# A planned TensorE stream: event waits counted in its instruction blocks, and tiling forms chosen by the tiling in force

## The chip, the cores and the metric

The kernel runs on one core of a Trainium2 chip (trn2). The metric is the time of one execution on the device in microseconds (us), as the median of several runs. Beside it stands one profiled execution, from which all rows and durations are taken; its times are in us unless marked ns.

## The reference

Two branches over the same input `x` (2048 tokens, 576 features) are mixed by a gate for each token.

```python
g = sigmoid((x * gate_w).sum(-1, keepdims=True))
a = A(x)      # recurrent, 64 segments of 32 tokens
b = B(x)      # full attention, 32 heads of 18 features
out = g * a + (1 - g) * b

# A: for each segment s (H = 32 heads of 128, M = 8 memory rows)
h = concat([mem, x_s])                     # 40 rows
q, k, v = h @ Wq, h @ Wk, h @ Wv           # 576 -> 32 x 128
p = softmax(mask(q @ k.T * scale))         # 40 x 40, each head
o = (p @ v) @ Wo
mem = o[:8]; out_s = o[8:]                 # the next segment needs mem

# B: qkv = x @ wqkv, softmax(q @ k.T * scale) @ v over 2048 x 2048, @ wo
```

The weights, inputs and the output are bfloat16. Branch A is a chain of 64 dependent segments, branch B is independent of it.

## The kernel before

**Tiling.** Features are cut in four pieces of 128 and a tail of 4 x 16 rows. Branch A's projections, one pair (q, k or v; half of the heads) at a time, are `Q0 Q1 K0 K1 V0 V1`: five groups of four matmuls, one for each group of 32 columns of TensorE's array ("column form", written 128\*32 in the profile), 512 wide, into `pvv` (L1255). The profile writes a matmul's form as active rows x columns: 128\*128 is the full form, 32\*128 the row form, 64\*128 the tall form.

**A segment** then goes: `pvv` is cast to `tm`; q and k are transposed by DMA (`tt`) and copied to `qk`; scores `psh` (`ph`, L1378, with the mask from `veil`, L1370); exponent on ACT (`xp`); sums over the keys `pss` (`sm`, L1402); reciprocal `rq`; the sums are spread to all rows `prb` (`bc`, L1428); the weights are multiplied (`nm`); values `pso` (`po`, L1450, tall form); copies to `ot`; output product `acc` (`op`, L1163); `oc`/`bd` prepare its first rows and `fold` (`fo`, L1507) turns them into the memory columns of the next segment's `ht` (`ph`, L1517). Only 32 of the 40 rows go through this path. The last 8 tokens of each segment are projected ahead in *last-token units* (`last_unit`, L1000 and L1004, into `pv`), two units a segment, for 16 segments at a time; their output product is `lo0`/`lo1` (`acc` from `otl`), once for four segments.

**Branch B** is 512 *visits*: four heads' scores at once in row form (`sb` and `sp`, L907), two exponents on ACT (`ex`, `ey`), and the values in column form (`ob`, L930). They are spread over the segments (`seg_gate`) to fill TensorE while a segment's chain waits.

**The order.** The kernel doesn't write its instructions in loops' order. Every step is added to a `Plan` with its engines, an assumed duration, dependencies, priority, tiling `mode`, PSUM banks it takes and gives, and, for TensorE, `pairs`, the number of its matmuls (each with a weight load). `Plan.run` is a list scheduler: it always places the step that can start first, with a priority among those within `near`, and `emit` then writes all instructions in that order. A change of TensorE's tiling is charged `SWITCH` = 0.105 us in the plan, and `rank` in `choose` adds the knob `switch` to the priority of a step in another tiling. `choose` waits for urgent steps by further knobs.

`TURNS` holds 65 seeds, one for each segment and one more; `turn` derives from a seed, through `factor`, a multiplier for the priority of each kind of step and for each of six knobs. They come from a search.

**Filler.** While branch B's accumulator is open and the plan sees TensorE idle for longer than 0.216 us plus the knob `gap`, it puts in a *warm* step: matmuls with zeros added onto `ob` (`warm_col`, L877, four 512 wide; `warm_full`, L883, one).

**Blocks.** `fetched` models that TensorE's instructions come in blocks of 128 pairs. `count` is the pairs placed so far; when a step crosses a block's end, it is set back until `FETCH` us after the last crossing:

```python
BLOCK, FETCH = 128, 3.75
for k in range(self.BLOCK - self.count % self.BLOCK, n + 1, self.BLOCK):
    at = start + dur * k / n + late
    late += max(0.0, self.block_end + self.FETCH - at)
    self.block_end = at
```

Event waits that the build puts into TensorE's stream as instructions of their own aren't in `count`.

**Forms.** Which form a step takes is fixed by constants, `LA_COL, SM_COL, BC_COL, FO_COL = False, True, True, True`: the sums, the spread and the fold in column form (4 x 3 matmuls), the last-token products of q and k in full form (5 matmuls of 128 columns for a part), those of v in column form except in the first group, before the segments.

Of the kernel before, what the change touches and what calls it, by code (L numbers as in the profile page):

```python
# [55 lines left out]
RANK = dict(RANKS[0])  # L56
TURNS = [
    7483491, 5720459, 7783898, 6678073, 6223742, 3115698, 6578494, 0, 354389, 7990747, 1981828, 1088679,
    6361070, 8635106, 9405432, 0, 1645198, 9020719, 1300847, 3314955, 2575603, 9878751, 9165885, 8658054,
    7165588, 8616252, 6219048, 2965226, 8978382, 6854479, 7325218, 5187600, 3485097, 1925321, 7771989,  # L60
    9649268, 8425308, 6353945, 3935120, 9399223, 8266427, 5356296, 6832100, 452821, 6190037, 6777369, 3367981,
    1424859, 9365357, 1390216, 6449117, 224178, 2255892, 1025974, 9211044, 7746781, 430414, 7144472, 1307610,
    6009236, 9165363, 683202, 7413963, 1206068, 9782046,
]
# [3 lines left out]

def factor(turn, k):
    h = (turn * 2654435761 + k * 40503 + 12345) & 0xFFFFFFFF  # L70
    h ^= h >> 15
    h = (h * 2246822519) & 0xFFFFFFFF
    h ^= h >> 13
    h = (h * 3266489917) & 0xFFFFFFFF
    h ^= h >> 16
    return FACTORS[(h >> 8) & 15] if turn and (h & 255) < 80 else 1.0

# [10 lines left out]
class Op:  # L88
# [3 lines left out]
        "engs", "dur", "fn", "deps", "prio", "mode", "take", "give", "tail",  # L92
        "eng", "start", "end", "left", "users", "name", "seq", "slots", "dmas", "kb", "use", "pairs", "kind",
    )
# [11 lines left out]
class Plan:  # L106
# [8 lines left out]
    WARM = 0.216  # L115
    BLOCK, FETCH = 128, 3.75
    ARRAY = {"col": 1.0, "row": 1.0, "full": 0.9, "half": 0.3, "tall": 0.35}
# [13 lines left out]
    def fetched(self, start, dur, n):  # L131

        late = 0.0
        for k in range(self.BLOCK - self.count % self.BLOCK, n + 1, self.BLOCK):
            at = start + dur * k / n + late
            late += max(0.0, self.block_end + self.FETCH - at)
            self.block_end = at
        self.count += n
        return late
# [24 lines left out]
    def add(  # L164
        self, name, engs, dur, fn, deps=(), prio=5.0, mode=None, take=(), give=(), tail=0.0, dmas=0, kb=0.0,
        use=None, pairs=4,
    ):
        op = Op(name, engs, dur, fn, deps, prio, mode, take, give, tail)
        op.dmas, op.kb = dmas, kb
        op.pairs = pairs  # L170
        op.kind = self.kinds.setdefault(kind_of(name), len(self.kinds))
        op.use = self.ARRAY.get(mode) if use is None else use
        op.seq = len(self.ops)
        op.slots = {}
        self.ops.append(op)
        return op

    def turn(self, k, stage):
        turn = TURNS[k]
        self.weight = [factor(turn, i) for i in range(len(self.kinds))]  # L180
        self.rank = {x: RANKS[stage][x] * factor(turn, 1000 + i) for i, x in enumerate(KNOBS)}

# [9 lines left out]
    def run(self):  # L192
        free = self.free = {e: 0.0 for e in ("PE", "DVE", "ACT", "POOL", "SP")}
        waiting = {e: [] for e in free}
        mode = None
# [9 lines left out]
        n = len(self.ops)  # L205
# [7 lines left out]
        while len(order) < n + extra:  # L213
# [10 lines left out]
            est, op = best[pick]  # L224
            if pick == "PE" and open_ and self.warm is not None:
                for m in ("col", "full"):
                    if m not in (mode, op.mode):
                        continue
                    turn = 0.0 if mode == m else self.SWITCH
                    done = sum(d for t, d in recent if t > free["PE"] - 2.5)  # L230
                    if est - free["PE"] < self.WARM + turn + self.rank["gap"] or done > self.rank["cool"]:
                        continue
                    w = Op("warm", "PE", self.WARM, self.warm[m], [], 9.0, m, (), (), 0.0)
                    w.dmas, w.kb, w.slots, w.left, w.use = 0, 0.0, {}, 0, 1.0
                    w.eng, w.start, w.end = "PE", free["PE"], free["PE"] + self.WARM + turn
                    w.end += self.fetched(w.start, self.WARM + turn, 4 if m == "col" else 1)
                    free["PE"], mode = w.end, m
                    recent.append((w.end, self.WARM))
                    order.append(w)
                    extra += 1  # L240
                    pick = None
                    break
                if pick is None:
                    dirty = {"PE"}
                    continue
# [8 lines left out]
            if pick == "PE":  # L254
                if op.mode != mode:
                    dur += self.SWITCH
                mode = op.mode
                if op in self.opens:
                    open_ = True
                if op in self.closes:  # L260
                    open_ = False
                recent = recent[-8:]
                recent.append((est, dur * op.use))
                dur += self.fetched(est, dur, op.pairs)
            op.end = est + dur
# [34 lines left out]
    def choose(self, e, ops, now, mode):  # L300
# [32 lines left out]
        def rank(f):  # L333
            op = f[1]
            switch = 0.0 if e != "PE" or op.mode == mode else self.rank["switch"]
            return (self.weighed(op) + switch, op.seq)
# [24 lines left out]
def kernel(  # L361
# [15 lines left out]
    nc = tc.nc  # L377
# [136 lines left out]
    ON_PE = ()  # L514
    LA_COL, SM_COL, BC_COL, FO_COL = False, True, True, True

# [481 lines left out]
    def tiled(q, out_, lw, rw, c, wide=False):  # L998
        if q == 0 or not (wide or LA_COL):
            nc.tensor.matmul(out_, lhsT=lw, rhs=rw, start=(c == 0), stop=(c == NF))  # L1000
            return
        for i in range(4):
            r = slice(32 * i, 32 * i + 32)
            nc.tensor.matmul(  # L1004
                out_[r, :], lhsT=lw[:, r], rhs=rw, start=(c == 0), stop=(c == NF),
                tile_position=(0, 32 * i), skip_group_check=True,
            )

    def last_unit(q, kind, b, prio, gate_dep):
# [21 lines left out]
        for k in range(NF + 1 if kind == 2 else NF):  # L1031
            a = add(
                f"la{tag}.{k}", "PE", 0.216 if kind == 2 else 5 * (0.062 if q and LA_COL else 0.057), part(k), [a] if a else deps,
                prio=prio - (0.01 if a else 0.0), mode="col" if q and (kind == 2 or LA_COL) else "full",
                take=() if a else ("pb",), pairs=(1 if kind == 2 else 5) * (4 if q and (kind == 2 or LA_COL) else 1),
            )
            parts.append(a)
# [147 lines left out]
    for s in range(n_seg):  # L1185
# [125 lines left out]
        for hf in range(2):  # L1311
# [82 lines left out]
            def sm(e, hf=hf, s=s):  # L1394
                box["pss", s, hf] = ps = bank([P, 6], FP32, "pss")
                for k, o in enumerate(CH):
                    if not SM_COL:
                        nc.tensor.matmul(
                            ps[:, 2 * k:2 * k + 2], lhsT=opened["et", hf][:, o:o + P], rhs=bsel[:, :], start=True, stop=True
                        )  # L1400
                    for i in range(4) if SM_COL else ():
                        nc.tensor.matmul(  # L1402
# [4 lines left out]

            s_ = add(f"sm{hf}.{s}", "PE", 0.08 if SM_COL else 0.1, sm, [x_], prio=RANK[f"sm{hf}"],
                     mode="col" if SM_COL else "full", take=("pb",), use=0.05, pairs=12 if SM_COL else 3)

# [7 lines left out]
            def bc(e, hf=hf, s=s):  # L1418
                box["prb", s, hf] = pr = bank([P, W8], FP32, "prb")
                for k, o in enumerate(CH):  # L1420
                    for jj in () if BC_COL else range(2):
                        nc.tensor.matmul(
                            pr[64 * jj:64 * jj + 64, o:o + P],
                            lhsT=box["rq", s, hf][:, 2 * k + jj:2 * k + jj + 1].to_broadcast([P, 64]),
                            rhs=ident[:, :], start=True, stop=True, tile_position=(0, 64 * jj),
                        )
                    for i in range(4) if BC_COL else ():
                        nc.tensor.matmul(  # L1428
# [5 lines left out]
            b_ = add(f"bc{hf}.{s}", "PE", 0.176, bc, [r_], prio=RANK[f"bc{hf}"],  # L1434
                     mode="col" if BC_COL else "half", take=("pb",), use=0.3, pairs=12 if BC_COL else 6)

# [6 lines left out]
            def pso(e, hf=hf, s=s):  # L1443
# [3 lines left out]
                for r in range(8):  # L1447
                    for jj in range(2):
# [6 lines left out]

            o_ = add(f"po{hf}.{s}", "PE", 0.2, pso, [n_, lv, *pvx], prio=RANK[f"po{hf}"], mode="tall", take=("pb", "pb"), pairs=16,
                     give=(("tm", evx, 0),))
# [36 lines left out]
        if s + 1 < n_seg:  # L1494
            def fold(e, s=s):
                box["pw", s] = pw_ = bank([P, NF + 2, M], FP32, "pw")
                obf, bd = box["obf", s], opened["bd"][:, :, :].rearrange("p a r -> p (a r)")
                for out_, lw, rw in (
# [3 lines left out]
                ):  # L1502
                    if not FO_COL:
                        nc.tensor.matmul(out_, lhsT=lw, rhs=rw, start=True, stop=True)
                    for i in range(4) if FO_COL else ():
                        r = slice(32 * i, 32 * i + 32)
# [4 lines left out]

            fo = add(f"fo{s}", "PE", 0.15 if FO_COL else 0.1, fold, [c1, c2], prio=RANK["fo"],
                     mode="col" if FO_COL else "full", take=("pb",), use=0.05, pairs=12 if FO_COL else 3)
            cur["fold"] = fo
# [235 lines left out]
```

## Time and profile before

| what | value |
|---|---|
| median of 3 runs | 1476.0 us (1470.29 to 1479.61) |
| profiled execution | 1476.89 us, span 1475.1 us |
| mean granted TensorE clock | 0.992 |
| TensorE matmuls | 35767, busy 1375.4 us |
| ACT busy | 1098.7 us (74%) |
| DVE busy | 775.5 us (53%) |
| POOL busy | 541.7 us (37%) |
| filler, 512 wide in column form | 800 matmuls |
| instruction fetch of TensorE (q8) | 279 packets, 4.57 MB |

The span is the time from the first to the last instruction of the profile. Matmuls overlap, since four column tiles run at once and a matmul's end is modelled: their busy time is not the time that they cost. What a matmul costs is read from the distance between two starts. In a row of the timeline stand start, duration, engine, line, the tile written and those read, the form, the shape and the count; a bracket gives idle time of the engine ahead of it and what ended it. "issue" there means that nothing the profile shows was waited for.

### The profile page before, as it was taken

What the parts mean: (1) busy time and instruction counts of PE and PEld (TensorE: products, weight loads), DVE (VectorE), ACT (ScalarE), POOL (GpSimd) and SP (SyncE); (2) the same over time, 40 slices, a digit from 0 to 9 for tenths busy, and PEclk for the clock granted to TensorE, in tenths of its full rate; (3) what the DMA queues carried; (4) which work ended last, traced back from release to release, by engine and by line L of the source; (5) the groups of instructions that cost most, each with busy time, mean ns of one, the idle gap of its engine ahead of it and who ended that gap; (6) DMA issues with size and microseconds to landing.
All of it is one profiled execution on the core that took longest, in us unless ns stands there. A gap on an engine that the chain in (4) does not pass through costs nothing. (4 is left out here: it accounts for less than half of the span.)

```text
span 1475.1 us, 79537 instructions
## 1 busy us (share of the span) xinstructions
PE 1375.4 (93%) x35767; PEld 753.3 (51%) x35767; DVE 775.5 (53%) x1856; ACT 1098.7 (74%) x1311; POOL 541.7 (37%) x1174
## 2 busy tenths in 40 slices
PE   7788999999999999999999999999999998989998
PEld 5345454555555544555555555545554444454445
DVE  6343465555555464555555564545554545545556
ACT  2167898897778787788777787777787777868784
POOL 6223254334532344332533335333353323422320
PEclk9999999999999999999999999999999999999999
DMA  8976543333333343332433334433334333343335
GB/s 254 324 236 202 103 80 74 63 68 68 77 58 68 60 84 66 69 63 61 85 59 71 63 67 72 75 54 66 59 76 84 58 52 54 68 57 53 53 71 172
DMA packets 343424, 130.79 MB, mean 89 GB/s; under 512 B 296943, under 2 KB 329159, under 8 KB 343083
## 3 DMA queue, kind: packets, MB, share of 16 engines
q1 hardware_dynamic: 314771, 81.20, 28.0%
q0 software_dynamic: 27088, 43.31, 11.2%
q8 instruction: 279, 4.57, 1.4%
q10 hardware_dynamic: 1224, 1.20, 0.3%
q14 instruction: 62, 0.51, 0.1%
HBM read 52.74 MB, written 30.86 MB: 57 GB/s over the span
## 5 line engine op out<-in xcount | busy, mean ns | idle before, releaser
L916 ACT ACTIVATE etb<-sb 128x1536 bf16<-128x1536 f32 x512 | 743.4, 1452 | 234.9 <-PE sp L907 184.8
L522 DVE CAST tm<-pvv 128x512 bf16<-128x512 f32 x343 | 236.3, 689 | 237.3 <-PE pvv L1255 233.8
L1255 PEld LDWEIGHTS <-ht 128*32 128x32 bf16 x7680 | 198.1, 96 | 223.8 <-issue 42.8
L920 ACT ACTIVATE etb<-sp 128x512 bf16<-128x512 f32 x512 | 304.9, 596 | 0.7 <-PE sp L907 0.7
L907 PE MATMUL sb<-qch,kch 32*128 32x512 bf16 x1536 | 201.6, 386 | 4.4 <-ACT etb L916 3.6
L930 PE MATMUL ob<-etb,vch 128*32 128x512 bf16 x2048 | 203.5, 384 | 1.5 <-issue 1.1
L907 PE MATMUL sp<-qch,kch 32*128 32x512 bf16 x512 | 197.3, 385 | 6.9 <-DVE wo L634 2.0
L1163 PE MATMUL acc<-wo,ot 128*32 128x144 bf16 x8192 | 169.1, 229 | 14.4 <-issue 12.4
L1163 PEld LDWEIGHTS <-ot 128*32 128x32 bf16 x8192 | 135.7, 98 | 45.3 <-issue 28.2
L1255 PE MATMUL pvv<-wk_m,ht 128*32 128x512 bf16 x2048 | 148.6, 381 | 0.5
L1255 PE MATMUL pvv<-wv_m,ht 128*32 128x512 bf16 x2048 | 145.0, 380 | 0.1
L1255 PE MATMUL pvv<-wq_m,ht 128*32 128x512 bf16 x2048 | 141.7, 381 | 2.7 <-DVE ht L1517 0.6
L522 DVE CAST ot<-pso 128x320 bf16<-128x320 f32 x200 | 91.9, 484 | 74.3 <-PE pso L1450 71.1
L907 PEld LDWEIGHTS <-kch 32*128 32x128 bf16 x2048 | 54.4, 91 | 140.8 <-issue 124.2
L1206 POOL COPY ht<-xg 128x96 bf16<-128x96 bf16 x64 | 18.0, 281 | 280.2 <-PE pvv L1255 243.5
L1355 DVE COPY qk<-tt 128x512 bf16<-128x512 bf16 x256 | 77.4, 306 | 49.7 <-DMA tt<-tm 46.2
L826 POOL DMA_DIRECT2D qch<-qtd x120 | 61.5, 519 | 96.7 <-PE sp L907 84.1
L930 PEld LDWEIGHTS <-vch 128*32 128x32 bf16 x2048 | 54.4, 94 | 58.3 <-issue 48.7
L1439 DVE TENSOR_TENSOR et<-et,prb 128x320 bf16<-128x320 bf16 x128 | 61.4, 484 | 42.5 <-PE prb L1428 34.6
L1388 ACT ACTIVATE et<-psh 128x320 bf16<-128x320 f32 x128 | 56.2, 443 | 36.6 <-PE psh L1378 33.8
L826 POOL DMA_DIRECT2D otd<-stage x124 | 63.1, 516 | 45.6 <-DVE stage L973 33.2
L522 DVE CAST vl<-pv 128x512 bf16<-128x512 f32 x78 | 53.4, 688 | 37.2 <-PE pv L1000 17.4
(154 smaller groups left out, 1957.9 us busy)
## 6 DMA issues: line engine op xcount, KB each, us to landing
xl<-qkd SPq DMA_DIRECT2D x64, 128.0 KB
v_sb<-tm SPq DMA_DIRECT2D x256, 32.0 KB
qkd<-vl POOLq DMA_DIRECT2D x48, 128.0 KB, 2.8
wo<-in_A_Wo_dram POOLq DMA_DIRECT2D x4, 1152.0 KB, 8.2
vgd<-vt SPq DMA_DIRECT2D x32, 128.0 KB
wv_m<-in_A_Wv_dram POOLq DMA_DIRECT2D x4, 1024.0 KB
wq_m<-in_A_Wq_dram POOLq DMA_DIRECT2D x4, 1024.0 KB, 8.9
wk_m<-in_A_Wk_dram POOLq DMA_DIRECT2D x4, 1024.0 KB
```

Source lines behind the costliest of these rows:

```text
L522: nc.vector.tensor_copy(out=out_of(), in_=in_of())
L826: dma(out=rows_, in_=pads) if out else dma(out=pads, in_=rows_)
L907: nc.tensor.matmul(sb[:, j, :] if j < 3 else sp[:, :], lhsT=kc[r, o:o + P], rhs=qt_[r, :], start=True, stop=True, tile_position=(32 * j, 0),)
L916: nc.scalar.activation(out=etb[:, 0:3, :], in_=box["sb", gq, kb][:, :, :], func=ACT.Exp, scale=scale_b)
L920: nc.scalar.activation(out=etb[:, 3, :], in_=box["sp", gq, kb][:, :], func=ACT.Exp, scale=scale_b)
L930: nc.tensor.matmul(ob[32 * j:32 * j + 32, :], lhsT=vc[:, o + 32 * j:o + 32 * j + 32], rhs=etb[:, j, :], start=(kb == 0), stop=(kb == NKB - ...
L1163: nc.tensor.matmul(acc[32 * j:32 * j + 32, :], lhsT=o[:, slot, t0:t0 + CT], rhs=wo[:, h, RW * j:RW * j + RW], start=(first and s_ == 0), s ...
L1206: nc.gpsimd.tensor_copy(out=ht[:, 0:NF, M:CT], in_=xg[:, 0:NF, t])
L1255: nc.tensor.matmul(pv[32 * j:32 * j + 32, :], lhsT=ht[:, cc, :], rhs=rw, start=(c == 0), stop=(c == NF), tile_position=(0, 32 * j), skip_g ...
L1355: eng.tensor_copy(out=opened["qk"][:, hf, a, 0:16 * L].rearrange("p (j i t) -> p j i t", i=4, t=L)[:, :, :, 0:CT], in_=box["tt", s, a, hf] ...
L1388: nc.scalar.activation(out=opened["et", hf][:, :], in_=box["psh", s, hf][:, :], func=ACT.Exp, scale=scale_a)
L1439: nc.vector.tensor_tensor(out=et[:, :], in0=et[:, :], in1=box["prb", s, hf][:, :], op=ALU.mult)
```

## The change

- `Plan.add` takes `alt`, another form of a step: its mode, duration and pairs. When the step is placed on TensorE, its own form is used unless the tiling in force differs from it and either is that of `alt` or a coin thrown by the seed for that kind of step (`prefers`, about 100 in 256) says `alt`. The step's function reads `plan.now.form`. Tiling changes are charged by the form taken, and `rank` charges none where either form fits.
- `alt` is given to the sums `sm` (full, 3 matmuls, assumed 0.17), the fold `fo` (full, 3, 0.17), the last-token parts of q and k (column, 20 for 5, 5 x 0.062), and those of v (full, 1 for 4). The spread `bc` remains in column form. The constants go.
- `po` gets `waits=0.15`, pairs added to `count` before its own; `FETCH` becomes 3.8; in `fetched`, the loop is written with `while`.
- `TURNS` has 65 new seeds. All knobs and priorities in `RANKS` are as before.

```diff
-    BLOCK, FETCH = 128, 3.75
+    BLOCK, FETCH = 128, 3.8
...
-        for k in range(self.BLOCK - self.count % self.BLOCK, n + 1, self.BLOCK):
+        k = self.BLOCK - self.count % self.BLOCK
+        while k <= n:
             at = start + dur * k / n + late
             late += max(0.0, self.block_end + self.FETCH - at)
             self.block_end = at
+            k += self.BLOCK
         self.count += n
...
+    def prefers(self, op):
+        return self.liked[op.kind]
+
     def turn(self, k, stage):
         turn = TURNS[k]
         self.weight = [factor(turn, i) for i in range(len(self.kinds))]
+        self.liked = [turn and (mixed(turn, 2000 + i) & 255) < 100 for i in range(len(self.kinds))]
...
             if pick == "PE":
-                if op.mode != mode:
+                pairs = op.pairs
+                if op.alt and mode != op.mode and (mode == op.alt[0] or self.prefers(op)):
+                    op.form, dur, pairs = op.alt
+                if op.form != mode:
                     dur += self.SWITCH
-                mode = op.mode
+                mode = op.form
...
-                dur += self.fetched(est, dur, op.pairs)
+                self.count += op.waits
+                dur += self.fetched(est, dur, pairs)
...
-            switch = 0.0 if e != "PE" or op.mode == mode else self.rank["switch"]
+            switch = 0.0 if e != "PE" or mode in (op.mode, op.alt and op.alt[0]) else self.rank["switch"]
...
-    LA_COL, SM_COL, BC_COL, FO_COL = False, True, True, True
...
-        if q == 0 or not (wide or LA_COL):
+        if plan.now.form == "full":
...
+                alt=None if not q else ("full", 0.216, 1) if kind == 2 else ("col", 5 * 0.062, 20),
...
-            s_ = add(f"sm{hf}.{s}", "PE", 0.08 if SM_COL else 0.1, sm, [x_], prio=RANK[f"sm{hf}"],
-                     mode="col" if SM_COL else "full", take=("pb",), use=0.05, pairs=12 if SM_COL else 3)
+            s_ = add(f"sm{hf}.{s}", "PE", 0.08, sm, [x_], prio=RANK[f"sm{hf}"],
+                     mode="col", take=("pb",), use=0.05, pairs=12, alt=("full", 0.17, 3))
...
-            o_ = add(f"po{hf}.{s}", "PE", 0.2, pso, [n_, lv, *pvx], prio=RANK[f"po{hf}"], mode="tall", take=("pb", "pb"), pairs=16,
+            o_ = add(f"po{hf}.{s}", "PE", 0.2, pso, [n_, lv, *pvx], prio=RANK[f"po{hf}"], mode="tall", take=("pb", "pb"), pairs=16, waits=0.15,
...
-            fo = add(f"fo{s}", "PE", 0.15 if FO_COL else 0.1, fold, [c1, c2], prio=RANK["fo"],
-                     mode="col" if FO_COL else "full", take=("pb",), use=0.05, pairs=12 if FO_COL else 3)
+            fo = add(f"fo{s}", "PE", 0.15, fold, [c1, c2], prio=RANK["fo"],
+                     mode="col", take=("pb",), use=0.05, pairs=12, alt=("full", 0.17, 3))
```

## The prediction

> **What bounds the kernel.** I read the page's busy row first, then the granted clock, the groups by form, the waits, and stretches of the timeline.
>
> ```profile
> PE 1375.4 (93%) x35767; PEld 753.3 (51%) x35767; DVE 775.5 (53%) x1856; ACT 1098.7 (74%) x1311; POOL 541.7 (37%) x1174
> PEclk9999999999999999999999999999999999999999
> q8 instruction: 279, 4.57, 1.4%
> ```
>
> TensorE is busy 93% at a granted clock of 0.99, so nothing is to be had from the clock. ACT is next with 74%. But busy is an overlapping measure, so I took each matmul's distance from one start to the next.
>
> ```profile
> 704.50 0.39 PE L1255 MATMUL pvv<-wq_t,ht 128*32 128x512 bf16 x4
> 704.72 0.39 PE L930 MATMUL ob<-etb,vch 128*32 128x512 bf16 x4
> 705.04 0.39 PE L907 MATMUL sb<-qch,kch 32*128 32x512 bf16 x3
> 705.05 0.38 PE L907 MATMUL sp<-qch,kch 32*128 32x512 bf16 x1
> 705.36 1.05 PE L1255 MATMUL pvv<-wk_m,ht 128*32 128x512 bf16 x16
> ```
>
> Four column tiles of 512 take 0.216 us (704.50 to 704.72). Where the tiling changes (128\*32 to 32\*128 and back), the same step takes 0.31 to 0.32: **a change of tiling costs 0.10 us**. With such steps for every form (a quad of 512 0.216, of `acc` 0.0625, `prb` 14 ns a matmul, `pss` 6.6, full-form `pv` 56) plus 0.10 for each of the 1383 tiling changes, TensorE's stream sums to 1296 us, of which 43.6 is filler on zeros (row L877: 800 matmuls; 2 in full form). The span is 1475.1. The other 179 us are stalls; some 40 of them lie in the first 200 us, 8 before the first matmul and after the last.
>
> One kind of stall has a period:
>
> ```profile
> 1140.96 0.49 PE L1163 MATMUL acc<-wo,otl 128*32 128x144 bf16 x19 [0.37 <-issue]
> 1141.38 0.37 PE L1450 MATMUL pso<-et,v_sb 64*128 64x40 bf16 x16
> 1141.68 0.40 PE L930 MATMUL ob<-etb,vch 128*32 128x512 bf16 x4
> 1141.91 0.31 PE L1370 MATMUL psh<-veil,ident 128*32 128x320 bf16 x4
> 1142.04 0.41 PE L1378 MATMUL psh<-qk 128*32 128x40 bf16 x32
> 1142.38 0.39 PE L907 MATMUL sb<-qch,kch 32*128 32x512 bf16 x3
> 1142.39 0.38 PE L907 MATMUL sp<-qch,kch 32*128 32x512 bf16 x1
> 1142.70 0.43 PE L1163 MATMUL acc<-wo,otl 128*32 128x144 bf16 x16
> 1143.02 0.24 PE L1402 MATMUL pss<-bsel,et 128*32 128x2 bf16 x12
> 1143.11 0.54 PE L1163 MATMUL acc<-wo,otl 128*32 128x144 bf16 x21
> 1144.98 0.37 PE L1163 MATMUL acc<-wo,otl 128*32 128x144 bf16 x11 [1.33 <-issue]
> ```
>
> From the stall before 1140.96 to that before 1144.98 stand 19+16+4+4+32+3+1+16+12+21 = 128 matmuls: with their weight loads 256 instructions, 2.5 us of work in 4.02 us, and the wait is for "issue", for no semaphore. The q8 row has 4.57 MB in 279 packets, 16 KB each: a block of 256 instructions. Cutting the program into such blocks at the place these stalls show, 92 blocks hold under 3.4 us of work (269.2 in sum) and took 344.6, 3.75 each; no block took under 3.0. **A block of TensorE's instructions costs about 3.75 us even when its work is shorter.**
>
> The Trainium skill speaks against this part of the change. Its page "Runtime: NRT & Kernel Launch", "Instruction fetch mechanics", has the same 16 KiB blocks but calls the fetch hidden behind the sequencer's issue, the crossing mostly free; by it, counting waits in blocks is worth 0. The rows give 75 us lost in 92 blocks. I follow the rows.
>
> **The change part by part**, by the instruction order of both kernels and the steps above.
>
> *Tiling in force.* 42 of 128 `sm` and 10 of 63 `fo` run in full form, 40 of the last-token parts (25 of wq, 15 of wk) in column form. Tiling changes fall from 1383 to 1323: 60 x 0.10 = **-6.0 us**.
> - Sums in full form: 3 matmuls of 128x2 for 12. No row has this; nearest is the gate's `pgs` (128x1, full), 25 ns each, so 75 ns against 79: 42 ops, -0.2 us. Upper end 56 ns each as full `pv`: +3.7. I take 0. The folds: 0.
> - Last-token products in column form: 200 full matmuls become 800. Row `prb` has this shape (128\*32, 128x128) at 14 ns, 56 a quad, as the full one's 56: 0. The skill says otherwise: "TensorEngine Tiling (Array Packing)", "Restrictions", has column tiling switch off fast weight loading, and "TensorE: Matmul & The Clock Gate", "LDWEIGHTS", sizes a load as its columns over 1.2, 27 ns for 32. Four in a row are 107 ns against 56: an estimate of +10 us over the 200 products. The trace shows that they don't run in a row:
>
> ```profile
> 700.20 1.17 PE L1163 MATMUL acc<-wo,ot 128*32 128x144 bf16 x64
> 701.20 0.39 PE L877 MATMUL ob<-unit,nil 128*32 128x512 bf16 x4
> ```
>
> 64 `acc` matmuls, each with its own 32-column load, in 1.00 us: 62.5 ns a quad, not 107. I take 0.
>
> *Order searched anew.* The filler falls from 200 quads and 2 full ones to 146 and 1. Filler goes where the plan sees TensorE idle for long enough, so this says that the new plan has fewer holes. But a few drawn thresholds ("gap") are higher now; without the stretches under those it is 164.5 to 120.3, 44 fewer. 44 x 0.216 = **-9.6 us**; if all count, -11.9; if the hole stays under the filler taken out, 0. All eight stages of eight segments but one have fewer.
> Beside TensorE, DVE takes 8 copies into `v_sb` from POOL (row L1294, 0.28 us on DVE) and 9 casts from ACT (row L522, 0.69): 8.5 us more over the whole run. DVE is busy 53%, so 0; without that cover a cast on a segment's chain costs its 0.69. The DMAs are the same in number on every queue, none is moved to another.
>
> *Waits in blocks.* 66 stand-alone event waits stand in TensorE's stream, 39 of them at L1450 (`po`); each takes an instruction's place, and the old plan counted none. So its blocks end up to 6 pairs off until segment 16, 10 off by segment 31, 15 to 19 off in the last sixteen. The new plan counts 0.15 pair for each `po` and stays within 4 after the start. No row prices this; it is bounded by the dense blocks. The shortfall of the programs' blocks below 3.75 us: before, 41.8 us in the first five stages of eight segments and 41.8 in the last three; after, 50.7 and 38.1. Really lost in the dense blocks before: 31.9 (0.76 of the shortfall) and 43.5 (1.04). If both ratios stay, 78.3 against 75.4: **+3**. If the late ratio is the drift's and falls to 0.76: 67.5, **-8**. The late stages also have fewer last-token products to put between, which the change leaves, so I take a value short of half way to the gain's end: **-2**.
> FETCH from 3.75 to 3.8 lies within what the blocks show: 0.
>
> **Sum**: -6.0 - 9.6 - 2 = -17.6 us. The profiled execution took 1476.9 (span 1475.1 and 1.8 around it), so 1459.3; the median of the three runs is 0.9 lower, so **1458**. What is late next is a segment's own chain: projection, cast, transposing DMA (3 to 4.5 us), scores, exponent, sums, products, fold.
>
> **Rivals.**
> 1. *The phase was the late stages' loss.* All the filler counts, and the late blocks lose no more than the early ones: -6.0 - 11.9 - 8 = -26, **1450**. For it: the loss rises from 0.76 to 1.04 of the shortfall as the count goes wrong. Against it: filler is thickest there too (94 of 200 quads in the last sixteen segments), so that these have holes from the chain.
> 2. *The chain holds the time.* Filler stood in real waits, and with it gone TensorE idles for as long: -6.0 + 3 = -3, **1473**. The new order is then better in the plan alone. For it: by the waits view DVE waited 46.2 us for the transposes (`qk` for `tt`), and some 100 us of stalls lie outside the dense blocks. Against it: the holes became fewer in seven of eight stages.
> 3. *Slower: column products starve the fetch.* They add 600 pairs, 4.7 blocks, as dense as `acc`. At 3.75 us a block they cost 17.6, the sums at their upper price 3.7, the unchanged ratios 3, and the filler gains nothing: -6.0 + 24.3 = +18, **1494**. It decides once some nine tenths of these pairs fall into blocks that are under 3.75 us already. Against it: 378 pairs of sums, 90 of folds and 217 of filler go, so that the program is 85 pairs shorter, and the shortfall over all blocks grows by 5.2 us only.
> That the change does not do what it says is excluded for the forms and the count: the order shows both. Whether the search found a better order is what rival 2 doubts.
>
> **From this to the numbers.** Forecast 50% (its own range 1452 to 1466), rival 1 20%, rival 2 22%, rival 3 8%. The three runs spread over 0.6%, so a measurement tells about 1% (14.8 us, under 1461 or over 1491) from no change. Faster by more: some seven tenths of the forecast, rival 1, and a little of rival 2, whose waits may shorten: 0.58. Slower by more: 0.06, most of rival 3. The rest, 0.36. The range goes from 1445, under rival 1 by the share of its terms that could still be larger, to 1474, rival 2's.
>
> **What would show it.** Right: about 35682 matmuls, L877's group at 584 in column form and some 50 us busy, tiling steps of still 0.31, the total of "issue" waits before `acc` (20.6 us now) smaller and the last three stages (950 to 1440 us now) shortened most. Full-form `pss` near 25 ns a step and `pv` quads at 56. Wrong: the same idle of TensorE with less filler (rival 2), or `pv` in 128\*32 with "issue" ahead of it (rival 3). Column quads far over 56 ns would overturn the price of the tiling part.

## The result, and the profile after

The changed kernel takes 1457.9 us in the median of four runs (1454.52 to 1462.65) against 1475.0 for the kernel before: a ratio of 0.9886 with a 95% interval of 0.9843 to 0.993, so faster by 1.1%. The profiled execution took 1456.2 us, with a span of 1454.3.

The busy row, the granted clock and the fetch row of its page:

```profile
PE 1353.4 (93%) x35682; PEld 745.6 (51%) x35682; DVE 786.2 (54%) x1873; ACT 1095.3 (75%) x1302; POOL 540.2 (37%) x1166
...
PEclk9999999999999999999999999999999999999999
...
q8 instruction: 279, 4.57, 1.4%
```

TensorE is as busy as before in share; it has 85 matmuls fewer and as many packets of instructions to fetch, and the granted clock is 0.996 for 0.992. The groups by form show the filler (L891) and the forms that are new (columns: line, engine, operation, tiles, form, shape and count, then busy us and mean ns, then idle ahead of it):

```profile
L891 PE MATMUL ob<-unit,nil 128*32 128x512 bf16 x584 | 50.9, 379 | 0.7 <-issue 0.7
...
L1413 PE MATMUL pss<-bsel,et 128*128 128x2 bf16 x126 | 9.2, 167 | 0.3 <-ACT et L1403 0.3
...
L1018 PE MATMUL pv<-xL,wq_m 128*32 128x128 bf16 x400 | 8.9, 219 | 0.0
```

The filler is 146 quads for 200; the sums have 126 matmuls in full form, some of the last-token products run in column form. A stretch of TensorE's timeline after shows these forms at work, each chosen by its neighbour:

```profile
703.22 0.42 PE L1018 MATMUL pv<-xL,wq_m 128*32 128x128 bf16 x16
703.45 0.24 PE L1018 MATMUL pv<-xL,wq_t 128*32 128x128 bf16 x4
703.51 0.41 PE L1018 MATMUL pv<-xL,wq_m 128*32 128x128 bf16 x16
703.73 0.24 PE L1018 MATMUL pv<-xL,wq_t 128*32 128x128 bf16 x4
703.91 0.39 PE L921 MATMUL sb<-qch,kch 32*128 32x512 bf16 x3
703.92 0.38 PE L921 MATMUL sp<-qch,kch 32*128 32x512 bf16 x1
704.23 0.40 PE L1014 MATMUL pv<-xL,wq_m 128*128 128x128 bf16 x4
704.47 0.22 PE L1014 MATMUL pv<-xL,wq_t 128*128 128x128 bf16 x1
704.52 0.22 PE L1413 MATMUL pss<-bsel,et 128*128 128x2 bf16 x3
704.60 0.38 PE L1014 MATMUL pv<-xL,wq_m 128*128 128x128 bf16 x4
```

A last-token part of 20 column matmuls takes 0.29 us (703.22 to 703.51), one of 5 full ones 0.28 to 0.29: the same. Three sums in full form, between full products, take 0.08 (704.52 to 704.60) and change no tiling. Reading all such steps of the trace: a column product takes 14.0 ns a matmul, a full sum 26 ns in the median (25 to 29 in most, 38 to 40 in the others), a change of tiling still 0.10 us.

The waits view of TensorE (in a row: us in total, times, longest) has less "issue" ahead of `acc` than before (20.6 us there):

```profile
PE acc L1178 <- issue: 17.4, 24, 1.2
PE psh L1393 <- DVE qk L1370: 6.5, 13, 1.2
```

The same sums as in the prediction, over the new trace (all in us; work includes filler and 0.10 for each change of tiling; lost is the time of blocks with under 3.4 us of work, "dense blocks", beyond that work; shortfall is what the work of the blocks falls short of 3.75 us):

| | before | after | difference |
|---|---|---|---|
| work of TensorE's stream | 1295.6 | 1277.4 | -18.2 |
| of it, filler | 43.6 | 31.7 | -11.9 |
| of it, changes of tiling | 138.3 | 132.3 | -6.0 |
| stalls between the first and the last matmul | 171.9 | 169.2 | -2.7 |
| of them, lost in dense blocks | 75.4 | 72.7 | -2.7 |
| span | 1475.1 | 1454.3 | -20.8 |

### The profile page after: what moved, and what is told of

Same layout as the page of the kernel before. It is cut to its first block, busy times and chain, and to the rows that moved or that the text cites. A ratio compares the mean times of both kernels' runs of the same rounds, so it can differ in the third digit from the quotient of the medians.

```text
span 1454.3 us, 79317 instructions
## 1 busy us (share of the span) xinstructions
PE 1353.4 (93%) x35682; PEld 745.6 (51%) x35682; DVE 786.2 (54%) x1873; ACT 1095.3 (75%) x1302; POOL 540.2 (37%) x1166
## 4 chain that ended last, share of the span: by engine, by line
PE 68%; DMA 14%; DVE 8%; issue 5%; ACT 4%; POOL 1%; SPq 0%; DVEq 0%; ACTq 0%; POOLq 0%
PE pvv L1270 24%; PE acc L1178 10%; PE sb L921 9%; DMA tt<-tm 7%; PE ob L944 7%; PE pv L1014 3%; ACT etb L930 3%; PE pso L1459 3%; DMA vgd<-vt 2%; PE pv L1018 2%; DVE tm L536 2%; PE psh L1393 2%; PE prb L1437 2%; PE pq L726 1%; PE po L1682 1%
## 5 line engine op out<-in xcount | busy, mean ns | idle before, releaser
L930 ACT ACTIVATE etb<-sb 128x1536 bf16<-128x1536 f32 x512 | 743.8, 1453 | 228.1 <-PE sp L921 162.5
L944 PE MATMUL ob<-etb,vch 128*32 128x512 bf16 x2048 | 199.7, 384 | 1.1 <-DMA vch<-vgd 0.8
L944 PEld LDWEIGHTS <-vch 128*32 128x32 bf16 x2048 | 53.9, 94 | 49.6 <-issue 36.2
L840 POOL DMA_DIRECT2D kch<-ktd x112 | 57.2, 518 | 42.9 <-PE sp L921 36.7
```

What stands on the lines that cost most here:

```text
L840: dma(out=rows_, in_=pads) if out else dma(out=pads, in_=rows_)
L930: nc.scalar.activation(out=etb[:, 0:3, :], in_=box["sb", gq, kb][:, :, :], func=ACT.Exp, scale=scale_b)
L944: nc.tensor.matmul(ob[32 * j:32 * j + 32, :], lhsT=vc[:, o + 32 * j:o + 32 * j + 32], rhs=etb[:, j, :], start=(kb == 0), stop=(kb == NKB - ...
```

## The experiments

Each was timed against the kernel before on the same chip. The first four runs shared a chip, the next four a second, the last four a third; so ratios to the kernel before are compared, not times. Theory: the time is the stream of TensorE, with its blocks. Main rival: the segments' chain sets it, and the stream has slack.

**Forms taken back, order kept.** In the changed kernel, each step is written in its first form:

```diff
             self.now = op
+            if op.name != "warm":
+                op.form = op.mode
             op.fn(op.eng)
```

> The changed kernel's order of steps, but each step written in its first form again (sums and folds in 4 x 3 column matmuls, last-token products of q and k in full form). By count 1376 tiling changes instead of 1323, +5.6 us of work and changes in TensorE's stream, 132 pairs fewer, and, since the blocks then fall elsewhere than the plan counted, 106.8 us of shortfall below 3.75 us instead of 88.8. Theory of the prediction (tiling changes and blocks are on the path): +5.6 and 0.76 x 18 = +14, some 1477 us. Rival (the segments' chain holds the time, TensorE's stream has slack): under +4, 1458 to 1462. A third: the forms matter and the blocks don't: +6, 1464.

Measured 1.0033 (1.0017 to 1.0049) of before: all of the gain is gone, some 22 us against the changed kernel's 0.9886. In its trace the work is 5.6 us more, as counted, and the dense blocks lose 91.0 us instead of 72.7. The first theory holds, and the rival (under +4) falls. But three quarters of this loss are blocks that no longer end where the plan had them, so the run gives no price of the forms alone: that the 53 changes of tiling cost their 5.6 us of time is not shown apart.

**Filler made one column wide,** in the changed kernel and in the one before. The matmuls stay, so the blocks stay:

```diff
-    box["ob"][32 * j:32 * j + 32, :], ..., rhs=unit[:, :].unsqueeze(1).to_broadcast([P, 4, P]), ...
+    box["ob"][32 * j:32 * j + 32, 0:1], ..., rhs=unit[:, 0:1], ...
```

> The changed kernel with the 146 filler quads kept at their place and count, but one column wide instead of 512: 17 us less work in TensorE's stream, the same blocks and tiling changes; shortfall of blocks 100.7 us instead of 88.8. If filler costs its time: -17 and 0.76 x 12 = +9, so -8, 1450 us. If filler stands in holes that are there anyway: 0, 1458. If its work holds the TensorE clock up, the clock falls under 0.99 and the time grows.

> The kernel before, with its 200 filler quads one column wide instead of 512: 23.6 us less work in TensorE's stream; shortfall of blocks 99.4 us instead of 83.6. If filler costs its time: -23.6 and 0.76 x 16 = +12, so -11, 1464 us, and then much of the change's 17 us is filler left out. If it stands in holes that are there anyway: 0, 1475, and the change's gain is in the holes themselves. If it holds the clock up: slower, with a clock under 0.99.

Measured 0.9937 (0.9914 to 0.996) and 1.0008 (0.9986 to 1.0031): no gain in either. The work taken out was even more than expected: where nothing holds the next matmul, it follows a light quad after 25 to 29 ns, not after the 100 ns that had been counted. So 27 and 38 us went, not 17 and 24. What comes after the filler starts almost as late as with full filler. In the changed kernel:

```profile
213.15 0.40 PE L891 MATMUL ob<-unit,nil 128*32 128x512 bf16 x4
213.61 0.39 PE L921 MATMUL sb<-qch,kch 32*128 32x512 bf16 x3
```

With light filler:

```profile
216.02 0.19 PE L891 MATMUL ob<-unit,nil 128*32 128x1 bf16 x4
216.48 0.39 PE L921 MATMUL sb<-qch,kch 32*128 32x512 bf16 x3 [0.27 <-ACT etb L930]
```

Here 0.46 us pass from the filler's start to `sb` in both. Summed over all filler, these stretches are 53.4 us in the changed kernel and 47.8 with light filler, 67.1 and 58.0 in the kernel before. Of the 47.8 and 58.0, 44.3 and 55.5 end with a wait for DVE or ACT. In the waits view of the changed kernel with light filler,

```profile
PE psh L1393 <- DVE qk L1370: 9.8, 20, 1.1
PE pvv L1270 <- DVE ht L1526: 9.4, 28, 1.0
PE prb L1437 <- DVE rq L1429: 7.4, 16, 1.0
```

TensorE now waits 9.4 us for the next segment's `ht` ahead of `pvv`, where the changed kernel itself has

```profile
PE pvv L1270 <- DVE ht L1526: 2.5, 5, 1.0
```

So more than three quarters of the filler's work stands in holes of the segments' chain and costs nothing. From 200 to 146 quads these holes themselves shrank: with light filler, where they lie bare, from 58.0 us to 47.8.

The rest, 5.6 and 9.1 us, was saved where the filler stands, but does not show in the whole time. One thing that can have taken it is the clock. In the five executions with light filler the granted clock was 0.984 to 0.991, against 0.992 to 0.996 in the four of the changed kernel; in the twelve of the kernel before with light filler it was 0.975 to 0.987, against 0.986 to 0.994 in 24 with full filler. In the profiles it is not a little lower throughout, but half for stretches of 3.4 us: 58.9 us in all in the kernel before with light filler, 24.1 with full filler. This is one of them in the windows view of the former (a stretch, its length, the busy time and count of PE, PEld, DVE, ACT and POOL, then the clock, 0.50):

```profile
819.70:823.10 3.40, 3.40 (x77) 1.94 (x79) 1.14 (x3) 1.69 (x2) 2.38 (x4) 0.50 0.05 11
```

So filler on zeros also holds the clock up here, the third outcome that was named. How much of the 5.6 and 9.1 us the clock took and how much the denser blocks is not shown.

**Blocks moved by 64 pairs.** In the changed kernel, 64 small matmuls in the gate's step, before the segments:

```diff
         pgs = bank([P, NT], FP32, "pgs")
+        for _ in range(64):
+            nc.tensor.matmul(pgs[:, 0:1], lhsT=xT[:, 0, 0:P], rhs=gw[:, 0:1], start=True, stop=True)
```

> The changed kernel with 64 small matmuls (128x1, 25 ns each, 1.6 us in all) added in the gate's step, before the segments: the same order after them, but every block of 128 pairs ends 64 pairs off the plan's count. Shortfall by count 117.9 us instead of 88.8 (73.9 for 50.7 in the first five stages, 44.0 for 38.1 in the last three). Theory of the prediction (blocks cost 3.75 us and their place matters): 0.76 x 29 and up to 1.6 = +22 to +24, 1480 us, more of it in the first stages. Rival (the issue waits come from elsewhere, the count is worth nothing): at most +1.6, 1458 to 1460.

Measured 1.0142 (1.0106 to 1.0178), 2.6% over the changed kernel's ratio: 38 us for 1.6 us of work. Nothing else in the order differs. A stretch of it in this run:

```profile
752.86 1.45 PE L1180 MATMUL acc<-wo,otl 128*32 128x144 bf16 x80
754.11 0.34 PE L1387 MATMUL psh<-veil,ident 128*32 128x320 bf16 x4
754.25 0.37 PE L1395 MATMUL psh<-qk 128*32 128x40 bf16 x29
756.75 0.20 PE L1395 MATMUL psh<-qk 128*32 128x40 bf16 x3 [2.13 <-issue]
756.76 0.45 PE L1180 MATMUL acc<-wo,otl 128*32 128x144 bf16 x16
757.13 0.39 PE L923 MATMUL sb<-qch,kch 32*128 32x512 bf16 x3
```

and the same matmuls in the changed kernel:

```profile
724.91 1.45 PE L1178 MATMUL acc<-wo,otl 128*32 128x144 bf16 x80
726.15 0.34 PE L1385 MATMUL psh<-veil,ident 128*32 128x320 bf16 x4
726.29 0.42 PE L1393 MATMUL psh<-qk 128*32 128x40 bf16 x32
726.52 0.45 PE L1178 MATMUL acc<-wo,otl 128*32 128x144 bf16 x16
726.90 0.39 PE L921 MATMUL sb<-qch,kch 32*128 32x512 bf16 x3
```

A group of 32 matmuls is cut after 29, in mid-flow, and TensorE waits 2.13 us for no semaphore; from `acc` to `sb` it is 4.27 us for 1.99. This is the fetch stall isolated.

Its place can be checked in every trace. Number TensorE's instructions through the program, two for each matmul and one for each event wait that stands alone. In the fourteen traces, 618 "issue" waits of over 0.15 us stand ahead of a matmul. Of these, 615 lie at one place in a block of 256 instructions, within two instructions: 46 of 46 in the kernel before, 35 of 35 in the changed one, 54 of 54 here. Without the event waits in the count, the place drifts by 19 matmuls over the kernel before. So the stalls come from the blocks, and event waits do take places in them.

The size was underestimated (22 to 24 us expected): dense blocks lost 111.5 us instead of 72.7, 0.95 of their shortfall by count instead of 0.82. A reading, not shown by a run: in a plan that knows its blocks, waits of the chain and waits for instructions fall together; moved, they add up.

**A drift put back, and one taken out.** In the changed kernel one sum's matmul is written twice in 23 of the 64 segments:

```diff
-                    if plan.now.form == "full":
+                    extra = 1 if hf == 0 and k == 0 and (s + 1) * 23 // 64 > s * 23 // 64 else 0
+                    for _ in range(1 + extra) if plan.now.form == "full" else ():
...
-                    for i in range(4) if plan.now.form == "col" else ():
+                    for i in [0] * extra + [0, 1, 2, 3] if plan.now.form == "col" else ():
```

> The changed kernel's order and forms, with one sum's matmul written twice in 23 of the 64 segments, evenly spread (0.6 us at most in all). That puts its blocks out of the plan's count as slowly as the uncounted waits did in the kernel before: from 4 pairs one way to 19 the other at the end. Shortfall below 3.75 us by count 91.0 us against 88.8. Theory (waits in blocks must be counted; -2 us in the prediction's sum, bounds +3 and -8): +2 to +8, 1460 to 1466. Rival (a drift of so few pairs is worth nothing): 0 to +1, 1458.

Measured 0.9948 (0.9919 to 0.9977). It lies above the changed kernel's 0.9886 as the theory wants, but the intervals overlap, and in its profile the dense blocks lose 71.8 us, not more than the 72.7. That is inconclusive.

The kernel before, with 113 of the gate's small matmuls added as above, which brings its late blocks to the plan's count and its early ones away from it:

> The kernel before, same order, with 113 small matmuls added in the gate's step (25 ns each, 2.8 us): its blocks end 15 pairs earlier, so that the last three stages stand within 4 pairs of the plan's count and the first five are 5 to 26 pairs off. Shortfall in the last three stages 37.4 us instead of 41.8, in the first five 47.5 instead of 41.8. Theory: the last three stages lose 4 to 10 us less, the first ones 5 us more and up to 2.8 for the added matmuls; whole time 1470 to 1478. Rival (late losses are the chain's): last three stages unchanged, time +3 to +8.

Measured 1.0002 (0.9978 to 1.0025). Lost in the dense blocks of the last three stages: 35.0 us instead of 43.5; of the first five: 39.4 instead of 31.9. So a part of the late loss was the drift's, some 8 us, and it was moved, not won. That is the one direct sign of what the drift costs, and it comes from one profile each; both have two stretches at half clock in the last three stages, so the clock does not make the difference.

**Seeds exchanged.** First the kernel before with the new `TURNS`, then the changed one with the old `TURNS` (there the last-token parts of v also lose their second form, which neither kernel uses):

```diff
-TURNS = [7483491, 5720459, 7783898, ...]
+TURNS = [4631337, 8646187, 1378870, ...]
```

> The kernel before with the changed kernel's 65 seeds: its forms, its count without waits, an order that nobody searched for. By count 1386 tiling changes, 230 filler quads, 1301.9 us of work, 94.8 us of block shortfall; the kernel before has 1383, 200, 1295.6, 83.6. If the seeds alone were good ones: 1458. If seeds are good only with the plan they were drawn for: +6 of work, +9 of blocks, 1485 to 1500.

> The changed kernel with the 65 seeds of before (and no second form for the last-token parts of v, which neither kernel uses): both forms allowed, waits counted, an order that nobody searched for. By count 1280 tiling changes, 229 filler quads, 1291.2 us of work, but 156.8 us of block shortfall, since the seeds ask for many more column products (38180 pairs). If the forms and the count bring the gain by themselves: 1458 or less. If blocks and search rule: -4 of work and 0.8 x 73 of blocks, 1515 to 1540.

Measured 1.0145 (1.0109 to 1.018) and 1.0406 (1.0374 to 1.0437). In both exchanges the seeds lose: here they are good for the plan that they were drawn with, and not for the other. The second has 2500 more pairs than the changed kernel, above all column products of the last tokens (3400 for 800), and is 5% over it by the ratios, though the changes of tiling fall to 1280. There "issue" stands ahead of the column products themselves, as the slower rival had it:

```profile
PE acc L1178 <- issue: 22.8, 34, 1.7
...
PE pv L1018 <- issue: 11.5, 13, 1.8
```

**The same search for four plans.** With seeds drawn afresh for each: with and without second forms (`alt=None`), with and without counted waits (`waits=0.15`, `FETCH` 3.8 against 3.75). All else is the changed kernel's, but that the v parts have no second form.

> Neither second forms nor counted waits (the plan of before, FETCH 3.75), with 65 seeds drawn by a search of one's own: beam of six, about 600 draws a segment, the same for this run and the next three. Count: 1393 tiling changes, 240 filler quads, 1304.8 us of work and changes, 83.5 us of block shortfall. In the runs so far the time is that work + 0.86 of the shortfall + 106 us (kernel before 1473, changed one 1460, seeds exchanged 1489 and 1532, blocks shifted 1486). So 1482 us. It is the base for the next three.

> Waits counted and FETCH 3.8, no second forms, the same search. 1383 tiling changes, 231 filler quads, 1301.9 us of work, 86.1 us of shortfall: 1482 us by the sum. If counting carries the change's gain: 8 to 15 us under the run with neither, since the blocks then lie where the plan has them. If it is worth little: within 3.

> Second forms for sums, folds and last-token products of q and k, waits not counted, the same search. 1316 tiling changes, 206 filler quads, 1289.5 us of work, but 108.6 us of shortfall, since 102 last-token parts are in column form (54 products of 5, four for one, instead of none): 1489 us by the sum. If forms carry the gain by themselves: 10 to 15 us under the run with neither. If the blocks take it back: 5 to 8 over it.

> Second forms and counted waits, the same search: the changed kernel's plan with seeds of a shallower search. 1321 tiling changes, 196 filler quads, 1287.8 us of work, 108.5 us of shortfall: 1487 us by the sum. If the changed kernel owes its 1458 to its plan and not to its seeds: 1458 to 1465.

(54 last-token parts are in column form in the third run; 102 is its number of full-form sum matmuls.)

| second forms | waits counted | ratio to before | interval |
|---|---|---|---|
| no | no | 1.0019 | 1.0 to 1.0038 |
| no | yes | 1.0057 | 1.0031 to 1.0083 |
| yes | no | 1.0101 | 1.0052 to 1.0149 |
| yes | yes | 1.0137 | 1.0078 to 1.0196 |

After a search that is the same for all four, and shallower than the one behind the changed kernel, neither part gives a gain. The forms cost 0.8%: by count they save 14 to 15 us of work and changes of tiling, and the blocks' shortfall grows (108.6 us for 83.5 without counted waits). Each cell is one set of seeds, and how far two draws for one plan differ was not measured; so differences of half a per cent may be luck of the draw, and the 0.8% may be in part.

**All kernels in one sum.** Work + 0.86 of the shortfall + 106 us, which was fitted to the runs before the last four, so that these four alone test it, beside the measured ratio times 1472 us (about the mean of the medians of before, 1468.9 to 1475.0):

| kernel | work | shortfall | sum | measured |
|---|---|---|---|---|
| before | 1295.6 | 83.6 | 1473 | 1472 |
| changed | 1277.4 | 88.8 | 1460 | 1455 |
| forms taken back | 1283.0 | 106.8 | 1481 | 1477 |
| light filler, changed / before | 1260.3 / 1272.0 | 100.7 / 99.4 | 1453 / 1463 | 1463 / 1473 |
| moved 64 / drift / moved 113 (before) | 1279.0 / 1277.8 / 1298.4 | 117.9 / 91.0 / 84.9 | 1486 / 1462 / 1477 | 1493 / 1464 / 1472 |
| new seeds, old plan / old seeds, new plan | 1301.9 / 1291.2 | 94.8 / 156.8 | 1489 / 1532 | 1493 / 1532 |
| searched: none / count / forms / both | 1304.8 / 1301.9 / 1289.5 / 1287.8 | 83.5 / 86.1 / 108.6 / 108.5 | 1483 / 1482 / 1489 / 1487 | 1475 / 1480 / 1487 / 1492 |

The sum is within 8 us for all but the two with light filler, which are 10 over it, because most of their missing work is no missing time; with the light quads at their real step they would be further over. For the last four it has the size, but not the order: by the sum "forms" is slowest and "count" fastest, by measurement "both" and "none".

## Why the prediction was right

- **What bounds.** TensorE's stream with its blocks, as forecast; the moved blocks and the place of the stalls show it. The clock has a little in it: half clock for 24.1 us of the profile before, so at most 12 us.
- **Tiling, -6.0.** The count and the step of 0.10 us hold in the trace after; that they make 6 us of time is not shown apart from the blocks. The prices of the new forms, 0, hold: column products 14.0 ns as taken from `prb`, full sums 26 ns in the median for 25. The +10 us that the Trainium skill's loading rule would give with loads one after another ("TensorE: Matmul & The Clock Gate", "LDWEIGHTS") are not there.
- **Order, -9.6.** The stream holds 11.9 us less filler, the upper value named, not the middle one (44.2 x 0.216 is 9.5, a slip of 0.1): the size was a little small, the reading right. Fewer quads were a gain because the holes shrank; light filler shows that most of the filler cost nothing where it stood.
- **Waits in blocks, -2.** The dense blocks lost 2.7 us less: 36.5 for 31.9 in the first five stages, 36.2 for 43.5 in the last three. By ratio to the shortfall that is 0.72 and 0.95: in the last stages between the ends that were named (0.76 and 1.04), in the first a little under. How much of it the counting did is only half shown: the drift put back did not resolve, and the profile before has two stretches of 3.4 us at half clock in the last three stages, the one after none, which can make up to 3.4 of the 7.3 us. That -2 came so near -2.7 is in part luck.
- **Sum.** -17.6 forecast. By the profiled executions it was -20.7 (1476.9 to 1456.2), by the medians -17.1; the interval is 6 us to either side, so the agreement within 1 us is closer than the runs can tell. Some of the 20.7 may be the clock's (0.996 for 0.992): over 73 executions of the kernel before, 0.01 of granted clock goes with 6 to 13 us, an estimate of 2 to 5 us here. A higher clock alone does not give the gain: with the forms taken back it was 0.994 in the mean of twelve executions, and the gain was gone.
- **Rivals.** In the first rival (1450), all the filler did count, but the loss in the late blocks fell to 0.95 of the shortfall, not to 0.76. The chain holding the time (1473) was right that filler stands in real waits, but with the new order these waits became shorter: stalls fell by 2.7 us, where that rival had them grow. Starved fetch (1494) appears where the seeds ask for 2500 more pairs; with the seeds chosen, 40 column parts did not bring it: `pv` in column form waited 0.4 us for "issue" there, 11.5 with the seeds of before.
- **A sign that was weaker than forecast.** The last three stages were to shorten most. They went from 507.6 to 497.7 us, the first five from 960.0 to 949.1: more per stage in the last, but about as much in sum, and the second stage alone (161.1 to 155.0) gave 6 of it.
- **Stays open.** Why the change's seeds reach an order that neither plan reached in the short search: it takes 40 column parts where the searched ones took 54 and 66. Which of the forms, the count and the longer search made the gain was not separated; what is shown is that none of the parts gives it without seeds chosen for it.

## What to carry to other kernels

When TensorE's program is long and made of small matmuls, cut it into blocks of 256 instructions, event waits included, and add up what each block falls short of the time that a block takes (here 3.75 us): in these runs this sum told of stalls that no semaphore shows. To find the blocks, look whether waits without a releaser recur at one place in 256 instructions. An order found by search belongs to its plan: 64 small matmuls cost 2.6%, so an edit should be followed by a new search before its worth is judged. Filler in a trace measured the holes here; before it is removed, look at what ends the wait behind it, and at the clock.

## What the runs showed of the hardware that was not expected

- 64 small matmuls (1.6 us) ahead of an unchanged order cost 38 us by moving where the instruction blocks end; 615 of 618 waits for no semaphore stand at one place in a block of 256 instructions.
- Four column tiles with a 32-column load each start every 56 ns for 128 moving columns, as fast as one full matmul (56 ns). The cost of column form showed in the instruction blocks.
- Cutting 512-wide filler to one column took out 27 and 38 us of array work and saved no time; the granted clock fell from 0.990 to 0.982 (means over 24 and 12 executions of the kernel before).
